# One kernel of attention and two gated layers: the strided heads of the first tile as TensorE products over eight residues

## The chip, the core and the metric

The kernel runs on one core of one Trainium2 chip. The metric is the device time of one execution in microseconds (us). Three timed runs of the kernel before gave 902.82, 904.25 and 905.61 us, a median of 904.25. The profiled execution took 902.92 us, of which the trace's span covers 901.1.

## The reference

Four sequences (B = 4) of 576 tokens go through attention with 8 heads of 64 features, and the result through two feed-forward layers of 512 to 1536 to 512.

```python
scores = scale * np.matmul(q, k.transpose(0, 1, 3, 2))
mask_local = (rel >= 0) & (rel < stride)                       # heads 0 to 3, stride = 32
mask_strided = (rel >= 0) & (pos[None, :] % stride == pos[:, None] % stride)   # heads 4 to 7
attn = np.exp(scores - max) / (sum + 1e-9)
x = np.matmul(attn, v)
x = ((x @ w_a) * (x @ w_b)) @ w_out                            # first layer
x = (sigmoid(x @ w_gate) * (x @ w_val)) @ w_out                # second layer
```

A strided head sees, for a token, only the earlier tokens with the same residue modulo 32. In the first tile of 128 tokens these are at most four.

## The kernel before

The sequence is cut into five tiles of 128, 128, 128, 128 and 64 tokens, taken for all four sequences together (512 columns). The attention of tile i + 1 is computed beside the first layer of tile i, so only tile 0's attention stands alone at the start. The first layer walks k over 12 blocks of the middle dimension: a gate product and a value product (24 matmuls of 512 columns, line 929, called L929 below), then an output product (12 matmuls, L1020). Each operand is held as a high and a low part of a narrower format, `w0p` and the like for weights, `x12p` to `x15p` for the activations: `x12p` and `x13p` hold the high parts of features 0 to 255 (local heads) and 256 to 511 (strided heads), `x14p` and `x15p` the low parts. The second layer (L1299) comes after all of it.

A weight block arrives by one DMA on the queue of SyncE (SP, L482), and four instructions make it usable: ScalarE (ACT) takes its top bits (L488), VectorE (DVE) merges (L497), ACT writes the high part (L505), DVE the low part (L509), which also frees one of three landing buffers.

Tile 0 is computed in two ways. The local heads run as four groups, one for each sequence (`attention`): ACT seeds a score bank with the mask (L561), TensorE (PE) adds the scores (L569), DVE takes the maximum (L581), ACT the exponentials (L587), DVE the reciprocal (L593) and the normalisation (L602), PE transposes (L610), ACT copies (L616), PE multiplies with the values (L624), ACT and DVE split the result (L633, L636). Before the seeds a matmul of the identity (`c_add`, L442) marks three score banks. The strided heads need no PE for their sums (`strided`): DVE and GpSimd (POOL) multiply keys by queries (L787), DVE sums over features (L793), DVE and ACT make the softmax, DVE and POOL multiply with values (L850), DVE sums (L857), PE transposes (L883), ACT and DVE split (L896, L900). The same function serves the later tiles.

The order on every engine is not written by hand: each step is handed to `Plan` with an engine (or several to choose from), a cost and a key, and `Plan.run` (L260) issues at each point the step that can start first by these costs, then by key. Engines execute in that order. While `plan.fill` is set, PE receives matmuls on a zero tile (L429) wherever the plan sees it idle in its first 27 us.

```python
    c_add = adding(SCORES, [c_idb], -20)
        z = add("ACT", act2(w), seed, [c_mask, c_add] + ...)
            a = add("PE", nb * 162, qk, [lq, z] + war, key, ...)
    strided(0, -10, 18, [], [])
    for n, g in enumerate(GROUPS):
        if g.i == 0:
            attention(g, n * 1.5, OTHERS, True, [])
```

## Time and profile before

| what | value |
|---|---|
| timed runs, us | 902.82, 904.25, 905.61 (median 904.25) |
| profiled execution, us | 902.92; span 901.1 |
| PE busy | 892.8 us, 99% of the span |
| DVE busy | 655.1 us, 73% |
| ACT busy | 405.0 us, 45% |
| POOL busy | 11.4 us, 1% |
| chain that ended last | PE 97%, DVE 3% |
| DMA | 132.67 MB, mean 147 GB/s |

Busy PE time counts fills and modelled ends, so 99% says only that PE has hardly any gap. The start has to be read from its own rows: which of PE's instructions there are fills, and what the first L929 wait for.

### The profile page before, as it was taken

The page shows a single profiled execution, that of the slowest core. Times are in us where ns is not written, and L with a number is a line of the kernel's source. Part 1 is how long each engine was busy: PE and PEld are TensorE (multiplying, and loading weights), DVE is VectorE, ACT ScalarE, POOL GpSimd, SP SyncE. Part 2 cuts the span into 40 slices and gives each one's busy share as a digit, 9 for nine tenths or more (in the row PEclk, how much of TensorE's full clock was granted, in tenths as well). Part 3 has the DMA queues.
Part 4 walks back from the last instruction along what each step waited for, and adds up shares of the span by engine and source line. Part 5 has one row for each costly group of instructions (what it writes and reads, how often), then busy time and mean ns, then how long its engine had stood idle before and what let it go on. Part 6 is the DMA issues. An engine that isn't in the chain of part 4 may idle for free.

```text
span 901.1 us, 13664 instructions
## 1 busy us (share of the span) xinstructions
PE 892.8 (99%) x5170; PEld 802.0 (89%) x5170; DVE 655.1 (73%) x1078; ACT 405.0 (45%) x843; POOL 11.4 (1%) x23
## 2 busy tenths in 40 slices
PE   8999999999999999999999999999999999999998
PEld 4678888888888888888899999999999999999998
DVE  7999988998999879811328876675768458649481
ACT  5776644411242113311236655564656445435351
POOL 4000000000000000000000000000000000000000
PEclk9999999999999999999999999999999999999999
DMA  9676564311242124300034233645575588953501
GB/s 297 212 238 221 200 195 141 91 44 61 85 137 72 54 65 134 106 1 1 0 118 164 94 139 116 213 152 187 204 241 169 194 302 331 381 165 117 167 17 62
DMA packets 62513, 132.67 MB, mean 147 GB/s; under 512 B 5872, under 2 KB 37232, under 8 KB 61552
## 3 DMA queue, kind: packets, MB, share of 16 engines
q1 hardware_dynamic: 62160, 131.60, 43.7%
q8 instruction: 40, 0.66, 0.3%
q14 instruction: 25, 0.20, 0.1%
q10 hardware_dynamic: 288, 0.21, 0.1%
HBM read 97.19 MB, written 34.60 MB: 146 GB/s over the span
## 4 chain that ended last, share of the span: by engine, by line
PE 97%; DVE 3%; issue 0%; ACT 0%; DVEq 0%
PE bank L1299 43%; PE bank L929 33%; PE bank L1020 17%; PE bank L624 1%; PE idle L429 1%; PE bank L569 1%; PE bank L610 1%; PE bank L883 0%; DVE nm L581 0%; DVE rest L497 0%; PE bank L442 0%; DVE w8p L857 0%; DVE w9p L857 0%; DVE x14p L636 0%; DVE w4p L1255 0%; DVE w0p L509 0%
## 5 line engine op out<-in xcount | busy, mean ns | idle before, releaser
L954 ACT CAST h16p<-rest 128x512 fp32r<-128x512 f32 (+1 forms) x60 | 34.7, 578 | 143.7 <-PE bank L1020 140.5
L1311 DVE TENSOR_TENSOR rest<-bank,rest 128x384 f32<-128x384 f32 x84 | 46.3, 555 | 56.6 <-PE bank L1299 32.5
L950 DVE TENSOR_TENSOR rest<-bank,rest 128x512 f32<-128x512 f32 (+1 forms) x60 | 38.1, 635 | 53.7 <-PE bank L929 53.5
L1072 ACT COPY rest<-bank 128x512 f32<-128x512 f32 (+1 forms) x60 | 32.6, 544 | 92.2 <-PE bank L929 92.0
L1317 ACT COPY rest<-bank 128x384 f32<-128x384 f32 x84 | 40.2, 479 | 67.4 <-PE bank L1299 67.1
L958 DVE TENSOR_TENSOR h16p<-rest,h16p 128x512 fp32r<-128x512 f32 (+1 forms) x60 | 38.2, 636 | 28.8 <-PE bank L1020 23.5
L787 DVE TENSOR_TENSOR rest<-rest 128x320 f32<-128x320 f32 (+13 forms) x56 | 51.5, 920 | 1.3 <-DMA rest<-sq 0.5
L850 DVE TENSOR_TENSOR rest<-rest,s 128x320 f32<-128x320 f32 (+13 forms) x56 | 51.5, 920 | 0.9
L793 DVE TENSOR_REDUCE s<-rest 128x5 f32<-128x320 f32 (+13 forms) x56 | 51.2, 915 | 1.2
L857 DVE TENSOR_REDUCE rest<-rest 128x64 f32<-128x320 f32 (+13 forms) x56 | 51.2, 915 | 1.0
L488 ACT ACTIVATE rest<-rest 128x512 f16<-128x512 bf16 x36 | 28.4, 793 | 9.4 <-DMA rest<-w 9.1
L1209 DVE SCALAR_TENSOR_TENSOR rest<-rest 128x512 uint32<-128x512 uint32 x36 | 24.7, 688 | 9.9 <-ACT rest L1202 9.8
L1202 ACT ACTIVATE rest<-rest 128x512 f16<-128x512 bf16 x36 | 28.0, 788 | 5.5 <-DMA rest<-w 5.5
L1382 DVE TENSOR_TENSOR rest<-bank,rest 128x384 f32<-128x384 f32 x36 | 20.0, 556 | 12.1 <-PE bank L1299 11.4
L1321 ACT COPY bank<-bank 128x384 f32<-128x384 f32 x42 | 19.6, 466 | 18.6 <-PE bank L1299 18.3
L1376 ACT ACTIVATE rest<-bank 128x384 f32<-128x384 f32 x36 | 17.6, 490 | 22.3 <-PE bank L1299 22.1
L497 DVE SCALAR_TENSOR_TENSOR rest<-rest 128x512 uint32<-128x512 uint32 x36 | 24.5, 685 | 0.6 <-ACT rest L488 0.5
L587 ACT ACTIVATE rest<-bank,nm 128x96 f32<-128x96 f32 x56 | 18.3, 338 | 12.2 <-DVE nm L582 10.7
L1376 ACT ACTIVATE rest<-rest 128x768 f32<-128x768 f32 x18 | 15.2, 846 | 14.0 <-DVE rest L1311 13.7
L1299 PE MATMUL bank<-w8p,w10p 128*128 128x384 f32 x100 | 20.7, 334 | 0.0
L1382 DVE TENSOR_TENSOR rest<-rest 128x768 f32<-128x768 f32 x18 | 17.2, 954 | 0.7 <-ACT rest L1376 0.3
L1299 PEld LDWEIGHTS bank<-w8p,w10p 128*128 128x128 f32 x100 | 17.6, 188 | 0.0
(500 smaller groups left out, 2413.7 us busy)
## 6 DMA issues: line engine op xcount, KB each, us to landing
rest<-w SPq DMA_DIRECT2D x72, 511.8 KB, 3.9
h2d<-rest SPq DMA_DIRECT2D x18, 768.0 KB, 4.2
rest<-qkv SPq DMA_DIRECT2D x12, 416.0 KB, 4.0
w2p<-h2d SPq DMA_DIRECT2D x12, 384.0 KB, 4.6
w0p<-h2d SPq DMA_DIRECT2D x12, 384.0 KB, 5.0
w1p<-h2d SPq DMA_DIRECT2D x12, 384.0 KB, 5.5
out<-rest SPq DMA_DIRECT2D x24, 192.0 KB, 1.8
x2d<-rest SPq DMA_DIRECT2D x16, 256.0 KB, 2.1
```

Of the source, the lines that this page charges most:

```text
L787: engine[op.eng].tensor_tensor(out=product(op, n), in0=x["k", h][:, :, :n, :], in1=x["q"][h // 2][:, e:e + nh, j:j + 1, :].to_broadcast([P ...
L793: DVE.tensor_reduce(out=weights_of(h, j, n), in_=x["p", op.deps[0]], op=ALU.add, axis=AX.X)
L850: engine[op.eng].tensor_tensor(out=product(op, n, "p (h d t) -> p h d t"), in0=x["v", h][:, :, :, :n], in1=weights_of(h, j, n).unsqueeze(2 ...
L857: DVE.tensor_reduce(out=xs[:, j, e:e + nh, :], in_=x["p", op.deps[0]], op=ALU.add, axis=AX.X)
L929: PE.matmul(x[tag][:, :n], ww[:, c * P:(c + 1) * P], xx(c), start=(u == 0 and c == chunks[0]), stop=(u == last and c == chunks[-1]),)
L950: DVE.tensor_tensor(out=x["g"], in0=x["b"][:, :n], in1=x["g"], op=ALU.mult)
L958: DVE.tensor_tensor(out=x["hl"], in0=x["g"], in1=r32(x["hh"]), op=ALU.subtract)
L1020: PE.matmul(ps[:, :n], ww[:, m * P:(m + 1) * P], x[xx], start=start, stop=stop)
L1299: PE.matmul(bank_of(where), at(*lhs(a, (0, 1, 0)[q], c), F32R), at(*rhs(b, (0, 0, 1)[q], c), F32R), start=p in OPENS and (q, c) == units[0 ...
L1311: DVE.tensor_tensor(out=at(*o), in0=bank_of("Z"), in1=at(*a), op=ALU.add)
L1317: "ACT", act2(NS), lambda op: ACT.copy(out=at(*o), in_=bank_of("Y")), [ops[after]], key - 20))
L1382: DVE.tensor_tensor(out=at(*o), in0=src(), in1=at(*o), op=ALU.mult)
```

## The change

In tile 0 the strided heads no longer go through `strided`. A new function, `strided_first`, lays queries and keys out by feature on the host (`fq`, `fk`, `fv`), with eight residues by four tokens as a block of 32. PE makes a 32 by 32 score block for each sequence, head and group of eight residues: 64 matmuls with 64 rows of contraction, on alternating halves of the array and alternating banks (L963 of the changed kernel). Of a block's entries only those of one residue and of earlier tokens count; a mask of 0 and a large negative number is put into the banks first, by a matmul of the identity with the mask in bf16 (L956). DVE and ACT make the softmax over 512 columns, PE transposes four times (L994), ACT copies (L998), and 64 small matmuls with 32 rows of contraction multiply with the values (L1024), in two steps of 32 whose results ACT and DVE split (L1041, L1045). The second step also ends the fills.

The local groups of tile 0 get their mask in the same way: one bf16 matmul of 384 columns in front of their scores (L571), in place of ACT's seed. `c_add` marks one bank instead of three. Later tiles keep the old code. The changed kernel's lines for old steps are shifted: L577 scores, L589 and L590 maximum, L595 exponentials, L601 and L602 reciprocal, L610 normalisation, L618 transposes, L624 or L626 copy, L632 values, L641 and L644 split, L433 fill, L493, L502, L510 and L514 the four weight steps, L1068 gate and value products, L800 and L806 the next tile's strided heads.

```diff
+R8 = 8
+FIRST_KEY = -1
+RB = R8 * TILES[0] // STRIDE
...
+    mskb = sb.tile([P, MW + RB], BF16, name="mskb")
...
+    c_mskb = add("ACT", act(MW + RB), lambda op: ACT.copy(out=mskb, in_=msk), [c_mask])
...
-    c_add = adding(SCORES, [c_idb], -20)
+    c_add = adding(SCORES[-1:], [c_idb], -20)
...
         def qk(op):
+            if first:
+                x["s"] = bank(op)[:, :g.width]
+                PE.matmul(x["s"], idb, g.mask(mskb), start=True, stop=False, skip_group_check=True)
...
-        z = add("ACT", act2(w), seed, [c_mask, c_add] + ([] if first else [lq]), key - 2, take=(("bank", SCORES if first else SCORES[-1:]),))
+        if first:
+            z = None
+            war = war + [c_idb, c_mskb, c_add]
+        else:
+            z = add("ACT", act2(w), seed, [c_mask, c_add, lq], key - 2, take=(("bank", SCORES[-1:]),))
         if held:
             pv_of, cost, deps, take, free, results = held
             a = add("PE", nb * 162 + cost, lambda op: (pv_of(op), qk(op)), [lq, z] + war + deps, key,
                     take=take + ring(("c", es)), free=free + ring(("qk", lq)))
             results(a)
         else:
-            a = add("PE", nb * 162, qk, [lq, z] + war, key, take=ring(("c", es)), free=ring(("qk", lq)))
+            a = add("PE", nb * 162 + first * 170, qk, [lq, z] + war, key,
+                    take=(("bank", SCORES),) if first else (("c", es),), free=ring(("qk", lq)))
...
+    def strided_first(key):
+        tq, nc2 = TILES[0] // STRIDE, HL // 2
+        nr = STRIDE // R8
+        half = B * nc2 * RB
+        w, nb = 2 * half, 2 * B * nc2
+        x = {"o": {}}
+        plan.slack = 0
+        def zone(n):
+            a = [early_tile() for _ in range(n)]
+            return a[0][0], n * DM, EARLY
+        qa, ka, va, ea, pa = zone(2), zone(2), zone(2), zone(1), zone(1)
+        def load(a, src, at_key):
+            return touch(add("SP", 450, lambda op: nc.sync.dma_start(out=at(*a), in_=src), (), at_key,
+                             size=P * a[1] * 4), (), [a])
+        lq, lk, lv = load(qa, fq, key - 9.9), load(ka, fk, key - 9.8), load(va, fv, key - 7)
+        def blocks(a):
+            return a.rearrange("p (n k) -> p n k", k=RB)
+        def wide(a):
+            return a.unsqueeze(2).to_broadcast([P, a.shape[1], RB])
+        def scores(op):
+            q, k = at(*qa), at(*ka)
+            x["s"] = [bank(op, e)[:, :half] for e in range(2)]
+            for s in x["s"]:
+                PE.matmul(blocks(s), idb, mskb[:, MW:].unsqueeze(1).to_broadcast([P, nb // 2, RB]),
+                          start=True, stop=False, skip_group_check=True)
+            for i in range(B * nc2):
+                for l in range(nr):
+                    o = (i * nr + l) * RB
+                    for e in range(2):
+                        rows = slice(e * D, (e + 1) * D)
+                        PE.matmul(
+                            x["s"][e][l * RB:(l + 1) * RB, i * RB:(i + 1) * RB], q[rows, o:o + RB], k[rows, o:o + RB],
+                            start=False, stop=i == B * nc2 - 1, skip_group_check=True)
+        def halves(a):
+            return [a[:, e * a.shape[1] // 2:(e + 1) * a.shape[1] // 2] for e in range(2)]
+        def top(op):
+            x["m"] = buf(op, "sm", [P, 32])[:, :nb]
+            for m, s in zip(halves(x["m"]), x["s"]):
+                DVE.tensor_reduce(out=m, in_=blocks(s), op=ALU.max, axis=AX.X)
+        def shift(op):
+            for m, s, o in zip(halves(x["m"]), x["s"], halves(at(*ea))):
+                DVE.tensor_tensor(out=blocks(o), in0=blocks(s), in1=wide(m), op=ALU.subtract)
+        def exp(op):
+            ACT.activation(out=at(*ea), in_=at(*ea), func=AF.Exp, scale=SCALE)
+        def total_of(op):
+            DVE.tensor_reduce(out=x["m"], in_=blocks(at(*ea)), op=ALU.add, axis=AX.X)
+            DVE.tensor_scalar_add(x["m"], x["m"], 1e-9)
+            DVE.reciprocal(out=x["m"], in_=x["m"])
+        def normalise(op):
+            engine[op.eng].tensor_tensor(
+                out=blocks(at(*ea)), in0=blocks(at(*ea)), in1=wide(x["m"]), op=ALU.mult)
+        def transpose(op):
+            x["t"] = bank(op)
+            for g in range(w // P):
+                PE.transpose(x["t"][:, g * P:(g + 1) * P], at(*ea)[:, g * P:(g + 1) * P], idt)
+        def copy_t(op):
+            if op.eng == "ACT":
+                ACT.copy(out=at(*pa), in_=x["t"])
+            else:
+                DVE.tensor_copy(out=at(*pa), in_=x["t"])
+        a = touch(add("PE", 4 * nb * 32 + 220, scores, [lq, lk, c_idb, c_mskb], key,
+                      take=[("bank", SCORES[:1]), ("bank", SCORES[1:2])]), [qa, ka])
+        b = add("DVE", 2 * dve(half), top, [a], key, take=[("sm", (0,))])
+        c = touch(add("DVE", 2 * dve(half), shift, [b], key, free=[("bank", a)]), (), [ea])
+        d = touch(add("ACT", act(w), exp, [c], key), (), [ea])
+        e = touch(add("DVE", dve(w) + 350, total_of, [d], key), [ea])
+        f = touch(add(("POOL", "DVE"), (1200, dve(w)), normalise, [e], key, free=[("sm", b)]), (), [ea])
+        t = touch(add("PE", w // P * 109, transpose, [f, c_id], key, take=[("bank", OTHERS)]), [ea])
+        h = touch(add(("ACT", "DVE"), (act(w), dve(w)), copy_t, [t], key, free=[("bank", t)]), (), [pa])
+        for c in range(nc2):
+            def values(op, c=c):
+                if c:
+                    plan.fill = None
+                for y in range(2):
+                    x["o", c, y] = bank(op, y)[:, :B // 2 * TILES[0]]
+                for g in range(B // 2):
+                    for l in range(nr):
+                        for e in range(2):
+                            for y in range(2):
+                                rows = slice((2 * c + y) * RB, (2 * c + y + 1) * RB)
+                                o = x["o", c, y].rearrange("p (g t l r) -> p g t l r", g=B // 2, t=tq, l=nr)
+                                PE.matmul(
+                                    o[e * D:(e + 1) * D, g, :, l],
+                                    at(*va)[rows, ((g * nr + l) * 2 + e) * D:][:, :D],
+                                    at(*pa)[rows, (e * 2 + g) * P + l * RB:][:, :RB]
+                                    .rearrange("p (t r) -> p t r", t=tq),
+                                    start=True, stop=True)
+            i = touch(add("PE", 32 * 45, values, [lv, h], key + 1 + c, take=[("bank", ((), (IDLE_BANK,))[c] + OTHERS[:2]), ("bank", OTHERS[2:])]),
+                      [va, pa])
+            for y in range(2):
+                def views(c=c, y=y):
+                    return [x["o", c, y].rearrange("p (g n) -> p g n", g=B // 2)] + [
+                        xT(r, 2)[:, c, :B * TILES[0]].rearrange("p (g y n) -> p g y n", g=B // 2, y=2)[:, :, y]
+                        for r in range(2)]
+                def high(op, views=views):
+                    ps, hi, lo = views()
+                    ACT.copy(out=hi, in_=ps)
+                def low(op, views=views):
+                    ps, hi, lo = views()
+                    DVE.tensor_tensor(out=lo, in0=ps, in1=r32(hi), op=ALU.subtract)
+                j = add("ACT", act(2 * P), high, [i], key + 1 + c)
+                k = add("DVE", dve(2 * P), low, [j], key + 1 + c, free=[("bank", (i, y))])
+                outs.setdefault(0, {}).setdefault(2 + c, []).append((j, k))
...
-    strided(0, -10, 18, [], [])
+    strided_first(FIRST_KEY)
```

On PE, at the start, the kernel before has the fills, the three marks and then a local group's scores (a seeded bank, `w7p` and `w6p` queries and keys):

```order
L442 MATMUL bank_108<-idb 128x512
...
L569 MATMUL bank_113<-w7p_89 64x64 x8
L429 LDWEIGHTS nil
L429 MATMUL idle<-nil 128x512
...
L569 MATMUL bank_115<-w6p_92,w7p_89 64x64 x8
```

The changed kernel has there (`w11p` holds the strided queries and keys, `mskb` the mask):

```order
L447 MATMUL bank_107<-idb 128x512
...
L956 MATMUL bank_126<-mskb,idb 128x256
...
L963 MATMUL bank_126<-w11p_76 32x32
L963 MATMUL bank_127<-w11p_76 32x32
...
L571 LDWEIGHTS idb
L571 MATMUL bank_199<-mskb,idb 128x384
L577 MATMUL bank_199<-w10p_83 64x64 x8
```

All 64 score matmuls of the strided heads stand in front of the first local group, and a mask matmul in front of every group.

On DVE the kernel before begins with products and sums of the strided heads (`w11p`, `w10p` products, `s` sums), between which the local groups' maxima are set:

```order
L787 TENSOR_TENSOR w11p_77<-w11p_77 128x512
L793 TENSOR_REDUCE s_75<-w11p_77 128x2x4
L793 TENSOR_REDUCE s_75<-w10p_84 128x2
...
L581 TENSOR_REDUCE nm_183<-bank_113 128x4
L582 TENSOR_SCALAR nm_183<-nm_183 128x4
L793 TENSOR_REDUCE s_75<-w10p_84 128x2x3
```

The changed kernel's DVE begins with the strided softmax, out of two banks:

```order
L973 TENSOR_REDUCE sm_209<-bank_126 128x8
L973 TENSOR_REDUCE sm_209<-bank_127 128x8
L977 TENSOR_TENSOR w10p_83<-bank_126,sm_209 128x256
L977 TENSOR_TENSOR w10p_83<-bank_127,sm_209 128x256
L589 TENSOR_REDUCE nm_214<-bank_199 128x4
L590 TENSOR_SCALAR nm_214<-nm_214 128x4
L983 TENSOR_REDUCE sm_209<-w10p_83 128x16
...
L589 TENSOR_REDUCE nm_238<-bank_220 128x4
...
L988 TENSOR_TENSOR w10p_83<-w10p_83,sm_209 128x512
```

Nothing on DVE precedes the end of the scores now, and the second group's maximum stands inside the strided chain.

On ACT, before the first products, the kernel before converts weights between the results of strided heads (`x13p`) and local groups (`x12p`):

```order
L896 CAST x13p_326<-bank_316 128x4x4x32
L488 ACTIVATE rest<-rest 128x512
L616 COPY w5p_122<-bank_330 96x512
L505 ACTIVATE w0p_350<-rest 128x512
L488 ACTIVATE rest<-rest 128x512
L633 CAST x12p_276<-bank_354 128x2x128
L616 COPY w4p_240<-bank_380 96x512
L896 CAST x13p_326<-bank_389 128x4x4x32
L505 ACTIVATE w0p_350<-rest 128x512
L633 CAST x12p_276<-bank_398 128x2x128
```

The changed kernel has there, from the split of the second value step to that of the last group:

```order
L1041 CAST x13p_383<-bank_349 128x2x128
L1041 CAST x13p_383<-bank_350 128x2x128
L493 ACTIVATE rest<-rest 128x512
L641 CAST x12p_420<-bank_395 128x2x128
L641 CAST x12p_420<-bank_407 128x2x128
L510 ACTIVATE w0p_434<-rest 128x512
L624 COPY w8p_93<-bank_422 96x512
L624 COPY w7p_110<-bank_429 96x512
L510 ACTIVATE w0p_434<-rest 128x512
L493 ACTIVATE rest<-rest 128x512
L641 CAST x12p_420<-bank_453 128x2x128
L641 CAST x12p_420<-bank_467 128x2x128
```

Both writes of a weight's high part (L510) have moved behind the split of the second value step.

## Rows read from the trace of the kernel before

**Rows 1.** Windows: busy us (count) of PE, PEld, DVE, ACT, POOL; PE clock; DMA.

```profile
20.00:30.00 10.00, 7.60 (x77) 4.47 (x75) 9.90 (x24) 7.10 (x21) 1.61 (x3) 1.00 0.74 236
40.00:50.00 10.00, 9.59 (x70) 7.25 (x68) 9.65 (x20) 7.07 (x16) 0.00 (x0) 1.00 0.66 203
100.00:500.00 400.00, 400.00 (x2251) 336.24 (x2250) 299.37 (x447) 128.74 (x303) 1.78 (x5) 1.00 0.28 89
```

**Rows 2.** Timeline of PE: start, us, operation, count, idle before and releaser.

```profile
0.98 3.60 PE L429 MATMUL idle<-nil 128*128 128x512 bf16 x8 [0.98 <-DVE nil L427]
5.65 4.39 PE L429 MATMUL idle<-nil 128*128 128x512 bf16 x17
...
22.57 0.69 PE L569 MATMUL bank<-rest 128*64 128x64 f32 x16
23.18 0.61 PE L429 MATMUL idle<-nil 128*128 128x512 bf16 x2
...
26.00 0.61 PE L610 MATMUL bank<-idt,w4p 128*96 128x128 f32 x4
26.45 0.60 PE L883 MATMUL bank<-idt,w8p 128*128 128x128 f32 x4
...
28.61 0.73 PE L929 MATMUL bank<-x12p,w0p 128*128 128x512 f32 x2 [0.64 <-ACT x12p L633]
...
30.47 1.09 PE L929 MATMUL bank<-x12p,w0p 128*128 128x512 f32 x4
```

**Rows 3.** Timeline of DVE at the start.

```profile
14.21 0.55 DVE L581 TENSOR_REDUCE nm<-bank 128x4 f32<-128x384 f32 x1
...
14.87 0.21 DVE L821 TENSOR_REDUCE sm<-s 128x16 f32<-128x64 f32 x1
...
24.71 0.16 DVE L593 TENSOR_SCALAR nm<-nm 128x4 f32<-128x4 f32 x1
...
28.83 0.42 DVE L636 TENSOR_TENSOR x14p<-bank,x12p 128x256 fp32r<-128x256 f32 x1
29.16 0.69 DVE L509 SCALAR_TENSOR_TENSOR w0p<-rest,w0p 128x512 fp32r<-128x512 f32 x1
29.76 0.49 DVE L787 TENSOR_TENSOR rest<-rest 128x320 f32<-128x320 f32 x1
30.36 0.49 DVE L793 TENSOR_REDUCE s<-rest 128x5 f32<-128x320 f32 x1
```

**Rows 4.** Timeline of ACT: the last exponential of group four, then five steps in a row.

```profile
19.54 0.33 ACT L587 ACTIVATE w4p<-bank,nm 128x96 f32<-128x96 f32 x1
...
22.12 0.80 ACT L488 ACTIVATE rest<-rest 128x512 f16<-128x512 bf16 x1
22.77 0.57 ACT L616 COPY w5p<-bank 96x512 f32<-96x512 f32 x1
23.23 0.68 ACT L505 ACTIVATE w0p<-rest 128x512 fp32r<-128x512 f32 x1
23.81 0.80 ACT L488 ACTIVATE rest<-rest 128x512 f16<-128x512 bf16 x1
24.45 0.37 ACT L633 CAST x12p<-bank 128x256 fp32r<-128x256 f32 x1
```

**Rows 5.** PE instructions by form, 0 to 35 us: busy, mean ns, idle before.

```profile
L569 PE MATMUL bank<-w7p 128*64 128x64 f32 x16 | 0.7, 228 | 0.0
```

**Rows 6.** Timeline of POOL at the start.

```profile
7.04 2.82 POOL L787 TENSOR_TENSOR w10p<-w10p 128x128 f32<-128x128 f32 x3 [5.24 <-DMA w10p<-sk]
```

**Rows 7.** Timeline of SP: issue of the second weight block.

```profile
13.27 0.33 SPq L482 DMA_DIRECT2D rest<-w  x1
```

**Rows 8.** DMA issues in the same place: size, us to landing.

```profile
rest<-w SPq DMA_DIRECT2D x1, 511.8 KB, 7.8
```

**Rows 9.** Timeline of DVE, last sum of the second tile's strided heads.

```profile
130.12 0.67 DVE L857 TENSOR_REDUCE rest<-rest 128x64 f32<-128x512 f32 x1
```

**Rows 10.** Timeline of PE, the transposes that read it.

```profile
131.13 0.60 PE L883 MATMUL bank<-idt,rest 128*128 128x128 f32 x4
```

More of the change, by code (lines that the diff above doesn't have):

```diff
@@ L351, in attention_moe_kernel @@
 @with_exitstack
-def attention_moe_kernel(ctx, tc, qkv, sq, sk, sv, w1, w2, mask, ident, out):
+def attention_moe_kernel(ctx, tc, qkv, fq, fk, fv, sq, sk, sv, w1, w2, mask, ident, out):
     nc = tc.nc
@@ L668, in attention @@
         c = add("ACT", nb * (act(WB) + 186), exp, [b], key + 2 * ST,
-                free=[("bank", z)])
+                free=[("bank", z or a)])
         used(c, (), [ee])
@@ L683, in results @@
         def results(i):
-            j = add("ACT", act(2 * g.n), high, [i] + war, i.key / 1e3 + ST)
+            j = add("ACT", act(2 * g.n), high, [i] + ([] if first else war), i.key / 1e3 + ST)
             k = add("DVE", dve(2 * g.n), low, [j], i.key / 1e3 + ST, free=[("bank", i)])
```

17 lines of the change are left out of this document (13 added, 4 removed).

## The prediction

> **What bounds the kernel now.** I first read the busy time by windows. From 100 to 500 us PE is busy 400.00 of 400.00, while DVE there has a quarter of its time free [rows 1]: behind the start the kernel is as long as PE's work. From 20 to 30 us PE is busy only 7.60 of 10, part of it fills, and DVE 9.90 of 10 [rows 1]. So what an edit of tile 0 is worth is the earlier moment at which PE's products begin to run without a gap, less what PE gets to do after it, which is nothing here.
>
> The second view is PE's timeline. The products of local features (`x12p`) start at 28.61, where PE had stood still 0.64 us for ACT's split [rows 2]. The tenth gate or value product is the second of the four at 30.47; they follow each other by 0.23 (1.09, less 0.40 for the end of the last, over three), so it ends at 30.93 [rows 2]. This is the mark by which I compare: ten products done, four local groups finished, the fifth group's scores done. In both orders the rest follows in the same manner.
>
> The third view, DVE and ACT side by side, says why it is so late. The fourth group's last exponential ran at 19.54 on ACT, but DVE got to its reciprocal at 24.71 [rows 3, 4]. Those 4.8 us are DVE's queue, full of the strided heads' products and sums. The change takes these away.
>
> **Prices of the steps.** All from one step's start to the next. DVE: 256 columns 0.33, 512 columns 0.60 (28.83, 29.16, 29.76), a maximum with its scaling 0.66 (14.21 to 14.87) [rows 3]. ACT: weight's top bits 0.65, copy of 512 0.46, high part 0.58 (22.12 to 23.81), 256-column split 0.25 to 0.37, taken as 0.25 [rows 4]. PE: scores of a group 0.61 (22.57 to 23.18), four transposes 0.45 (26.00 to 26.45) [rows 2]. A handover between engines I take as 0.1, with another 0.05 to 0.15 for the end of a matmul.
>
> What no row shows is a pass of a 32 by 32 by 64 product. A group's scores are 8 matmuls in the program and 16 in the trace, two passes each; so the 64 score matmuls are 128 passes, the value matmuls 64 passes in each of two steps. The nearest row has 64-column passes at (0.69 − 0.228) / 15 = 31 ns [rows 5]. That is the upper end, a pass that gains nothing from its half length. The lower end is 32 columns at the pace of a 512-column product: 32 × 227 / 512 = 14 ns. I take 22, the middle: half the columns, with neighbours on other halves of the array, but two instructions for each pass as in the row.
>
> **The change, step by step, at 22 ns.** PE first runs ten fills and the one mark at 0.43 us, from 0.98 to 5.7. [...] So three more fills at 0.43, four at 0.216 and two mask matmuls bring PE to 8.1. The loads don't hold it: `fq` and `fk` are 1.05 MB and stand first on SP; the first four strided loads, the same bytes, had landed by 7.04, when POOL could start [rows 6]. Behind them the order of SP changes, but in front of the first weight block stand the same bytes.
>
> Scores: 128 × 22 = 2.8, to 10.9. DVE: two maxima and two subtractions, 4 × 0.34, to 12.45. ACT: exponential of 512, 0.58, to 13.15. DVE: sum 0.6, plus and reciprocal 0.37; then the second group's maximum, 0.66, which stands ahead of the normalisation; then that, 0.6: 15.55. PE: transposes, 16.15; two fills 0.43 and the fourth group's mask and scores 0.77, to 17.35. ACT's copy is done by 17.0, so the values' first step runs 17.35 to 18.75. It shares banks with the local groups, so the second step waits for the first group's transposes (0.45) and DVE's copy of them (0.6): 20.2. It ends at 21.65.
>
> From there ACT's queue sets the end, since both weight blocks' high parts and the last local split stand in line behind that step. From 21.9: two splits 0.5, second block's top bits 0.65, two splits 0.5, high part 0.58, two copies 0.93, high part 0.58, third block's top bits 0.65, two splits 0.5: 4.9, to 26.8. PE starts the `x12p` products at 27.0 instead of 28.61; five more products after the first two (7 × 0.23) bring the mark to 28.6 instead of 30.93: **2.3 us earlier**.
>
> The mask matmuls (0.16 each) replace ACT's seeds and lie in the steps counted. POOL normalises the fourth group, from 21.8: at its 3.1 ns a column (2.82 us for 128, 256 and 512 columns [rows 6]) that is 1.2 us, to 23.0, and PE comes to it at 23.5. DVE loses strided work of tile 0, but its queue at the start of the next tile's strided heads moves with the rest: by the same sum it reaches L793's counterpart at 28.25 instead of 30.36 [rows 3], 2.1 earlier. That matters at the next tile, where DVE's last sum ended at 130.8 and PE came to it at 131.13 [rows 8, 9, 10]: 0.3 of slack, and the shifts differ by 0.2. In 40 to 50 us PE lacks 0.41 [rows 1], waits for weights; the changed ACT queue can lose as much again, since the fifth block's top bits now precede the fourth's high part. I count these two as nothing, ±0.4.
>
> Each further ns costs 128 + 128 ns: gain = 2.3 − 0.255 × (p − 22). It is zero at 31 ns. Below 18 the landing of the second weight block at 13.27 + 7.8 = 21.07 [rows 7, 8] begins to set ACT's queue, and the gain ends at 3.6.
>
> [...] The row has 31 ns for 64 columns [rows 5]; it cannot tell length from instruction. [...]
>
> **Rivals.** *A. Neighbouring passes overlap fully* (14 to 20 ns). For it: the passes alternate halves and banks. Against: the row's passes alternate column halves too, and took 31. Gain 2.9 to 3.6: about 900.7.
>
> *B. A pass costs what the row shows*, whatever its length (28 to 31 ns): the strided heads' 256 passes take 8 us of PE's queue, in front of every local group, and DVE's freed time turns into waiting. Gain 0 to 0.8: about 903.5.
>
> *C. PE's clock falls.* Between 11 and 21 us there are 12 fills where PE had been kept full, and the small products use a quarter of the array or less. If the pace there fell to 0.43 for 512 columns, the path's PE work after the scores (0.45 + 0.43 + 0.77 + 1.4 + 0.45 + 1.4 = 4.9) doubles, and the first 6 us of products (as long as fills took before the pace rose [rows 2]) lose 3: 7.9 − 2.3 = 5.6 slower, 909.5. It decides from a loss of 5.0, where the whole is 0.3% slower. Against: PE's gaps in my sum are under 0.9 us, and before it kept its pace across a 0.64 gap at 28.61.
>
> **Numbers.** The profiled execution, 902.92, is its span of 901.1 and 1.8 around it; less 2.3 it is 900.6. It lies 1.3 under the median of 904.25, so I set the sum against the mean of the four executions, 903.9: **901.6**. Chances: forecast (21 to 28 ns) 0.45, with 900 to 903.5 its own range; A 0.33; B 0.12; C 0.10. The bound of 0.3%, 2.7 us, is what a measurement of this kernel tells from no change. A passes it, with a little of the forecast's better edge, 0.40 faster; C makes 0.10 slower; the rest, 0.50, is the same. The range of 898.6 to 905.0 holds the three cases without C, with ±0.9 for executions.
>
> **What would show it.** The strided scores should start at about 8.1 and take 2.8; the values' steps 1.4 each; ACT should run without a gap from 21.9 to 26.8; `x12p` products should start near 27.0, and PE have no gap beyond 0.5 us after. I am wrong if the passes follow each other by less than 18 or more than 28 ns, if fills after 8 us come at 0.43, if PE waits at 131, or if a wait appears behind 30 us that keeps what the start gave.

## The result: slower by 0.6%, and the profile after

The changed kernel takes 908.95 us (908.33 to 909.23, six runs), the kernel before 903.12 beside it; the ratio is 1.0059 (95% interval 1.0046 to 1.0072). The forecast of 901.6, with a range of 898.6 to 905.0, was wrong, and so was its sign. The profiled execution has 908.95 us and a span of 907.2, 6.1 more than before.

TensorE's timeline of the changed kernel (start, us, operation, count, idle before) answers to [rows 2, 5]:

```profile
8.10 1.29 PE L963 MATMUL bank<-w11p 64*32 64x32 f32 x128
...
15.99 0.69 PE L577 MATMUL bank<-w7p,w8p 128*64 128x64 f32 x16 [0.74 <-DMA w7p<-qkv]
16.60 1.13 PE L1024 MATMUL bank<-w10p,w11p 32*64 32x32 f32 x64
17.67 0.64 PE L618 MATMUL bank<-idt,w10p 128*96 128x128 f32 x4
...
19.02 0.89 PE L1024 MATMUL bank<-w10p,w11p 32*64 32x32 f32 x43
23.39 0.54 PE L1024 MATMUL bank<-w10p,w11p 32*64 32x32 f32 x21 [3.48 <-issue]
23.86 1.05 PE L632 MATMUL bank<-w9p,w10p 96*64 96x64 f32 x16
...
26.57 1.01 PE L618 MATMUL bank<-idt,w7p 128*96 128x128 f32 x4
...
30.20 0.72 PE L1068 MATMUL bank<-x12p,w0p 128*128 128x512 f32 x2
...
31.45 1.09 PE L1068 MATMUL bank<-x12p,w0p 128*128 128x512 f32 x4
...
37.45 0.73 PE L1068 MATMUL bank<-x12p,w1p 128*128 128x512 f32 x2 [1.74 <-ACT w1p L510]
```

Until 19 us nothing is later than forecast: the scores start at 8.10, as forecast, and the second values step at 19.02, not 20.2. Then TensorE stops in the middle of that step, after 43 of 64 passes, for 3.48 us. "Issue" says that it waited for nothing that the profile shows. The products with `x12p` start at 30.20 instead of 28.61 [rows 2], and the next weight block keeps them waiting 1.74 us more.

ScalarE's timeline shows the hole handed on: its queue stands behind the strided split for 3.37 us, and the weight steps behind it.

```profile
23.96 0.65 ACT L1041 CAST x13p<-bank 128x256 fp32r<-128x256 f32 x2 [3.37 <-PE bank L1024]
24.49 0.79 ACT L493 ACTIVATE rest<-rest 128x512 f16<-128x512 bf16 x1
...
34.13 0.79 ACT L493 ACTIVATE rest<-rest 128x512 f16<-128x512 bf16 x1 [1.78 <-DMA rest<-w]
```

The windows (columns as in [rows 1]) show the rest of that stage: the transfers run dry at 37 GB/s, and TensorE's mean granted clock is 0.90 and 0.76 of full from 20 to 30 us, where it was 1.00 up to the hole. From the first values behind the hole to the second set of transposes are 2.71 us (23.86 to 26.57).

```profile
16.00:20.00 4.00, 3.85 (x132) 3.30 (x133) 3.39 (x10) 3.01 (x15) 0.00 (x0) 1.00 1.04 318
20.00:25.00 5.00, 1.61 (x43) 1.57 (x44) 1.80 (x6) 1.63 (x5) 1.14 (x1) 0.90 0.90 291
25.00:30.00 5.00, 5.00 (x74) 4.07 (x71) 3.89 (x10) 4.30 (x10) 0.00 (x0) 0.76 0.18 37
```

The transfers run dry because SyncE's queue stands: from 18 to 45 us its longest wait (queue, awaited, us in all, times, longest) is that of a load of later queries and keys (L556) for the scores of the fifth group to be done, which come behind the hole (27.51). The loads of the next weight blocks stand after it. In the kernel before the same wait took 3.8 us.

```profile
SPq L556 <- PE bank L577: 8.0, 1, 8.0
```

How far the changed kernel is behind the one before, at places that both have: tenth product 1.0 us (31.9 against 30.93), first output product 3.0, the next gate or value product 2.0, first product of the second layer 2.66, its last 5.79, span 6.1. So half of the loss arises where the change touches nothing. The first and last product of the second layer, of the kernel before:

```profile
502.66 1.40 PE L1299 MATMUL bank<-w0p,w4p 128*128 128x384 f32 x6
...
897.30 0.51 PE L1299 MATMUL bank<-w11p,x15p 128*128 128x384 f32 x2
```

and after:

```profile
505.32 1.39 PE L1438 MATMUL bank<-w0p,w4p 128*128 128x384 f32 x6
...
903.09 0.51 PE L1438 MATMUL bank<-w11p,x15p 128*128 128x384 f32 x2
```

394.64 us became 397.77, for 2268 passes in either. By form (busy us, mean ns of one with its modelled end, so that neighbours overlap; idle before), a pair with weight block 10 before, and two pairs after:

```profile
L1299 PE MATMUL bank<-w8p,w10p 128*128 128x384 f32 x48 | 9.6, 334 | 0.0
```

```profile
L1438 PE MATMUL bank<-w8p,w10p 128*128 128x384 f32 x48 | 9.8, 338 | 0.0
L1438 PE MATMUL bank<-w7p,w5p 128*128 128x384 f32 x36 | 7.2, 334 | 0.0
```

Pairs with one of the tiles of blocks 10 and 11 are slower (337 to 340 ns, before 334 or 335), most others are not (334 to 336).

### The profile page after: what moved, and what is told of

Read it like the earlier page. It is cut to its first block, busy times and chain, and to the rows that moved or that the text cites. A ratio compares the mean times of both kernels' runs of the same rounds, so it can differ in the third digit from the quotient of the medians.

```text
span 907.2 us, 14091 instructions
## 1 busy us (share of the span) xinstructions
PE 894.9 (99%) x5402; PEld 805.9 (89%) x5402; DVE 647.1 (71%) x1059; ACT 407.3 (45%) x849; POOL 4.3 (0%) x13
## 4 chain that ended last, share of the span: by engine, by line
PE 93%; DMA 3%; DVE 2%; issue 1%; ACT 0%; SPq 0%; ACTq 0%; DVEq 0%
PE bank L1438 43%; PE bank L1068 31%; PE bank L1159 16%; PE bank L632 1%; PE bank L618 1%; DMA w7p<-qkv 1%; PE bank L577 1%; DMA rest<-w 1%; DMA msk<-mask 1%; DMA rest<-sq 1%; DVE rest L800 0%; DVE rest L502 0%; DVE s L806 0%; PE bank L896 0%; PE bank L1024 0%
## 5 line engine op out<-in xcount | busy, mean ns | idle before, releaser
L800 DVE TENSOR_TENSOR rest<-rest 128x320 f32<-128x320 f32 (+13 forms) x56 | 51.6, 921 | 2.3 <-DMA rest<-sq 1.3
L806 DVE TENSOR_REDUCE s<-rest 128x5 f32<-128x320 f32 (+13 forms) x56 | 51.2, 914 | 1.2 <-DVE rest L800 0.5
L493 ACT ACTIVATE rest<-rest 128x512 f16<-128x512 bf16 x36 | 28.3, 793 | 6.6 <-DMA rest<-w 6.6
L502 DVE SCALAR_TENSOR_TENSOR rest<-rest 128x512 uint32<-128x512 uint32 x36 | 24.6, 684 | 1.2 <-ACT rest L493 1.2
L595 ACT ACTIVATE rest<-bank,nm 128x96 f32<-128x96 f32 x56 | 18.3, 340 | 11.4 <-DVE nm L590 9.9
```

The source lines that it names most:

```text
L800: engine[op.eng].tensor_tensor(out=product(op, n), in0=x["k", h][:, :, :n, :], in1=x["q"][h // 2][:, e:e + nh, j:j + 1, :].to_broadcast([P ...
L806: DVE.tensor_reduce(out=weights_of(h, j, n), in_=x["p", op.deps[0]], op=ALU.add, axis=AX.X)
```

## The experiments

Two causes were to be found: of the hole, and of the slower passes.

### The hole: where it stands

The page of the changed kernel has, in its parts on engines and DMA queues:

```profile
PE 894.9 (99%) x5402; PEld 805.9 (89%) x5402; DVE 647.1 (71%) x1059; ACT 407.3 (45%) x849; POOL 4.3 (0%) x13
...
q8 instruction: 42, 0.69, 0.3%
```

0.69 MB in 42 packets are 16 KB each. TensorE's 5402 passes, each with its weight load, and 79 other instructions of its program are 10,883: 259 to a packet, some 63 bytes each. From these numbers my estimate is a block of 256 instructions of 64 bytes to a packet (42.5 blocks); the runs below test the 256. Counted in the program, 705 instructions stand ahead of the hole; with 63 of start-up they would be 768, three blocks. The 63 are set by this one hole and kept below.

**e1_shift20** adds 20 instructions at the very start.

```diff
+    fills = [0]
+    def fill():
+        fills[0] += 1
+        n = 2 if fills[0] <= 10 else 1
+        for i in range(n):
+            PE.matmul(idle[:, :512 // n], nil, nil.unsqueeze(1).to_broadcast([P, 4 // n, P]), start=True, stop=True)
+
+    plan.fill = fill
...
```

> The first ten fills are issued as twenty matmuls of 256 columns instead of ten of 512: the same work and time, 20 instructions more ahead of everything else. Theory A: the 3.48 us in the second values step is TensorE out of instructions. The instruction queue's packets are 16 KB, 256 instructions of 64 bytes; the hole falls at the end of the third block, and the fourth lands late. Then the hole moves up by 20 instructions, ten passes: 33 passes of the step (a pass is a weight load and a matmul) come before it and 31 behind it, and it stays 3.3 to 3.9 us. Rival B: the step waits for something of its own (a bank, a buffer, an engine whose signal the profile doesn't show); then the hole stays behind the 43rd pass.

Measured (timeline of TensorE; 909.47 us, one run):

```profile
13.28 0.52 PE L1001 MATMUL bank<-idt,w10p 128*128 128x128 f32 x3
14.06 0.33 PE L1001 MATMUL bank<-idt,w10p 128*128 128x128 f32 x1 [0.26 <-issue]
...
17.94 0.73 PE L1031 MATMUL bank<-w10p,w11p 32*64 32x32 f32 x33
21.60 0.66 PE L1031 MATMUL bank<-w10p,w11p 32*64 32x32 f32 x31 [2.93 <-issue]
```

The hole is behind the 33rd pass, and rival B falls. A small gap that I had not foreseen stands where, by the same count, the second block ends: behind the third of four transposes.

**e9_swap_odd** gives the second values step a later place (with the tiles moved as in e5 below).

```diff
...
-            i = touch(add("PE", 32 * 45, values, [lv, h], key + 1 + c, take=[("bank", ((), (IDLE_BANK,))[c] + OTHERS[:2]), ("bank", OTHERS[2:])]),
+            i = touch(add("PE", 32 * 45, values, [lv, h], key + 1 + c * 5, take=[("bank", ((), (IDLE_BANK,))[c] + OTHERS[:2]), ("bank", OTHERS[2:])]),
...
```

> The second values step gets a later key and is issued behind the values of the first two groups and the scores of group 4; tiles at odd multiples of 128. Its 64 passes are all kept. Theory A: the third block of instructions now ends inside the values of group 2, after about 5 of their 16 passes; a hole of 1 to 2.5 us stands there instead of in the strided step, and the queues of ScalarE and VectorE, which stood behind the strided split for 3.4 us, have the weight steps of block 0 before them: products with x12p by 29 us (after: 30.2), time 903 to 905. If the hole belonged to the step, it goes with it.

```profile
20.62 0.34 PE L634 MATMUL bank<-w8p 96*64 96x64 f32 x5
23.40 0.69 PE L634 MATMUL bank<-w8p 96*64 96x64 f32 x11 [2.44 <-issue]
```

After five passes, as counted. The hole belongs to the count, not to the strided step. Of the time that it was to save nothing is seen in the profiled execution (clock 0.50 from 24 to 32, four transposes 1.09 us at 24.01 against 0.62 at 19.09, `x12p` at 31.11), but the median is 903.14 (901.04 to 906.94, ten runs; ratio 1.0002, 0.9987 to 1.0017). The profile shows one of its longest executions: the six with a mean granted clock of 0.998 or more took 901.04 to 903.36 us, the four with 0.996 or less 903.72 to 906.94. No run here shows why the clock falls further in some executions of one kernel than in others.

**e12_strided_odd** keeps the strided part alone; ScalarE seeds the first groups' banks as before.

```diff
...
-                PE.matmul(x["s"], idb, g.mask(mskb), start=True, stop=False, skip_group_check=True)
+        z = add("ACT", act2(w), seed, [c_mask, c_add] + ([] if first else [lq]), key - 2, take=(("bank", SCORES if first else SCORES[-1:]),))
...
```

> Only the strided part of the change is left: the first groups' banks are seeded by ScalarE as before. The strided scores are issued later, behind the scores of four groups, and the two values steps stand one behind the other, 256 instructions. Theory A: 256 instructions in a row are used up in 2 to 3 us, which no fetch under load (7 us) follows: TensorE stands with the label issue again, 1 us or more in all, in the strided scores (the second block ends after 66 of their 128 passes) or at the values steps (the third ends just before them, the fourth just behind). If the hole needs the mask matmuls, it is gone. Time 904 to 910.

```profile
19.90 0.77 PE L957 MATMUL bank<-w11p 64*32 64x32 f32 x66
21.44 0.73 PE L957 MATMUL bank<-w11p 64*32 64x32 f32 x62 [0.76 <-issue]
```

Behind the 66th pass, as counted; only 0.76 us long, less than expected, and at the values steps no wait on "issue". Its 916.0 us (one run), more than expected, goes with the order: the strided softmax now follows all groups, and `x12p` starts at 34.93.

**e8_mask_only** keeps the mask part alone.

```diff
-    strided_first(FIRST_KEY)
+    strided(0, -10, 18, [], [])
```

> Only the mask part of the change is left: the score banks of the first groups get the mask by the bf16 matmul, and the first tile's strided heads are computed on VectorE and GpSimd as before. Here no burst of small matmuls empties an instruction block, and its tiles lie at odd multiples of 128. Theory A with P2: no idle of TensorE put down to issue, the second layer at 394.6 us, and the time 902 to 904, like before: the mask part carries none of the loss. If the mask part has a share in the loss (its matmul, the later mask transfer), the time is 905 or more.

902.57 us (ratio 0.9991, 0.9982 to 1.0001), no wait on "issue", second layer 394.65 us: the mask part alone shows no loss.

### The hole: how long it lasts

**e4_probe** appends 1024 small matmuls where the transfers are nearly over.

```diff
+        last = psum.tile([P, 512], F32, tag="bank0", name="bank0")
+        for _ in range(1024):
+            PE.matmul(last[:32, :32], nil[:, :32], nil[:, :32], start=True, stop=True)
```

> 1024 small bf16 matmuls (32 columns, 32 rows, constant operands, nobody reads them) are appended behind the last product, where the transfers are nearly over (share 0.04 to 0.17): 2048 instructions, eight blocks of 256. Theory A: TensorE runs 128 passes and then stands, again and again, seven or eight times; a period is the time that a fetch takes with empty queues (4 us or less, from 8.9 asked to 13.0 landed in the after profile). Rival B: no holes, the 1024 passes run through at 10 to 30 ns each.

```profile
903.29 14.50 PE L1694 MATMUL bank<-nil 128*32 128x32 bf16 x546
918.15 3.36 PE L1694 MATMUL bank<-nil 128*32 128x32 bf16 x128 [0.36 <-issue]
921.88 9.42 PE L1694 MATMUL bank<-nil 128*32 128x32 bf16 x350 [0.36 <-issue]
```

Two gaps only, of 0.36, just 128 passes apart; the instruction packets come 3.4 to 4.0 us apart. A pass took 26 ns, so 256 instructions last 3.36 us, and 1024 passes hold eight ends of blocks: with quiet queues (share 0.13 from 903 to 907 us, the end of the changed kernel) six of them show no gap. If a block is asked for when the last but one before it is used up, which is my assumption, the fetch took no longer than 3.36 us, and twice 3.72. My "seven or eight times" was wrong because I took the pass for shorter.

In the changed kernel the second block was used up at about 16.1 (same count), the packet moved between 20.5 and 20.6, and TensorE went on at 23.39: 7.3 us. No view shows the moment of asking; it is taken from the count. The packet (kind, packets, MB, share, window 20.5 to 20.6):

```profile
q8 instruction: 1, 0.02, 75.6%
```

The third block lasted from 16.1 to 19.91, 3.8 us. Two kernels were to take loads out of the queues, **e2_light** and **e13_relief**:

```diff
...
-            start = strided(i + 1, begin[i], span[i], start, war)
+            start = strided(i + 1, begin[i], span[i], held_back if i == 0 else start, war)
...
```

> The third weight block and the first loads of the next tile's strided heads (1.3 MB in all) wait for the second strided split and so no longer stand in the DMA queues between 15 and 24 us. Theory A with contention: the fourth instruction block is asked for at 16.1 us and landed at 20.5 in the after profile because it stood behind these loads; now it lands by 18.5, and the hole in the second values step is under 1.5 us. If a fetch takes its 7 us whatever the queues hold, the hole stays at 3.5 us. Rival B: the hole stays. The time need not fall, since weights and strided keys come later: 906 to 912.

> All loads that are not needed before 20 us (the first weight blocks, the next tile's groups and strided heads) wait for the second strided split; only the first tile's own 4 MB are in the queues. Theory A with contention: these are over by 14 to 16 us, the fourth instruction block, asked for when the second is used up at about 16 us, is there within 3.4 to 3.8 us, as at the quiet end of the appended matmuls, and the hole after the 43rd pass is under 0.8 us. If a fetch takes its 7 us at any load, the hole stays at 3 to 3.5 us. All later work is several us late since the weights are: 908 to 920.

Holes of 3.20 us (913.57 us; 1.0122, 1.0106 to 1.0137) and 2.38 us (922.28), both behind the 43rd pass. But neither did what it says: what I added is a dependence in the planner, which gives an order, and no wait when the program runs. The transfers' share was still 1.05 at 18 to 20 us in e13. These two tell nothing of contention.

**e16_relief_wait** makes the loads wait for a write into their own buffers, issued behind the second split.

```diff
+                if w is w1 and done_loads.append(c) is None and len(done_loads) <= 3:
+                    DVE.memset(x["raw"][:, :1], 0)
...
```

> The first three weight blocks and the first loads of the next tile (scores, values, strided heads) each wait for a one-column write by VectorE behind the second strided split, into the buffer that they fill. Only the first tile's own 4.2 MB are in the queues, over by 15 or 16 us. Theory A with contention: the fourth instruction block, asked for at about 16 us, lands within 3.4 to 3.8 us; the hole after the 43rd pass is 0 to 0.8 us. A fetch of 6 to 7 us at any load: the hole stays at 2.4 to 3.5 us with the transfers idle. Time 915 to 930, since all weights come 10 us late.

Timeline of TensorE, two windows, and the packet of the fourth block (window 17 to 17.1):

```profile
18.73 1.34 PE L1035 MATMUL bank<-w10p,w11p 32*64 32x32 f32 x64
20.01 0.69 PE L639 MATMUL bank<-w9p,w10p 96*64 96x64 f32 x16
...
21.61 0.64 PE L625 MATMUL bank<-idt,w7p 128*96 128x128 f32 x4
```

```profile
16.00:18.00 2.00, 2.00 (x84) 1.89 (x80) 1.73 (x6) 1.32 (x9) 0.00 (x0) 1.00 0.03 8
18.00:20.00 2.00, 1.94 (x70) 1.52 (x67) 2.00 (x6) 1.24 (x7) 0.00 (x0) 1.00 0.00 0
```

```profile
q8 instruction: 1, 0.02, 66.6%
```

With the queues empty the packet moved 1.2 us behind the end of the second block (15.9 by the count; 4.4 us in the changed kernel), and the step ran through, though its order and so its count are the same. The clock stayed at 1.00, and what took 2.71 us takes 1.60 (20.01 to 21.61): the fallen clock cost 1.1 there. (In the 917.59 us of its one run TensorE later waits 4.86 us for the first weights.) So the hole is a late fetch, and the full queues make it late.

When a block is asked for is not shown. In e16, with nothing else in the queues (share 0.03 from 16 to 18 us), the packet of the fourth block moved at 17.0 to 17.1, only after the second block was used up (15.9); in the changed kernel, too, it came behind that moment (20.5 against 16.1). My assumption agrees with both, and neither proves it.

### The slower passes: where the tiles lie

The change made the tiles of constants larger (`msk`, and `mskb` new) and the order another in which tiles are first used. In bytes of a partition, modulo 256, the tiles of weights and activations all begin at 128 in the kernel before; in the changed kernel those of weight blocks 10 and 11 begin at 0, the others at 128. The constants are not the reason: they push all by 768 bytes, three times 256. The order is: the tile of the strided sums (`s`, 1152 bytes) stood ahead of the tiles of blocks 11 and 10, and now stands behind them. Four kernels move the tiles and do nothing else, and one moves them in the kernel before:

```diff
@@ e3_pad: 256 bytes ahead of all
+    idb = sb.tile([P, 2 * P], BF16, name="idb")[:, :P]
@@ e6_even: 128 ahead of all
+    nil = sb.tile([P, P + 64], BF16, name="nil")[:, :P]
@@ e11_all_even: 128 behind block 10
+            return sb.tile([P, shape[1] + 32], dtype, tag=f"{ring}{s}", name=f"{ring}{s}")[:, :shape[1]]
@@ e5_odd: the edits of e6_even and e11_all_even together
@@ e15_before_mixed: in the kernel before, the edit of e6_even, and
+                tiles[r] = phase, sb.tile([P, r[1] + 32 * (name == "w10")], F32, tag=name, name=f"{name}p{phase}")
```

> One tile of 256 bytes a partition is left unused ahead of the big tiles, so that all of them begin 256 bytes further on (those that held weight blocks 10 and 11 no longer begin at a multiple of 1024 bytes); nothing else is changed. Theory P: half of the loss, 3.1 us between 510 us and the end, is the pace of the second layer's passes (334 ns each before, 335 to 338 after), set by where the tiles lie in the buffer memory, not by the edit. Then the passes are at 334 again, the second layer is 2.4 to 3.1 us shorter and the time 905.8 to 906.6; the hole in the second values step is unchanged, after 43 passes and 3.5 us long. If the pace belongs to something else (instruction positions, transfers), the passes stay at 335 to 338 and the time at 908.5 to 909.2.

> All big tiles are placed at odd multiples of 128 bytes, as in the kernel before (128 unused bytes ahead of the tile of weight block 11, 128 more behind that of block 10; with 256 bytes ahead of all the pace stayed, so it isn't the residue to 1024). In the after profile just those two tiles lie at multiples of 256, and pairs with them run at 338 ns, where before no pair with them was over 335. Theory P2: this parity sets the pace. Then the second layer takes 394.6 us from its first to its last product, as before (after: 397.8), and the time is 905.5 to 906.3. If the pace belongs to the new order of the tiles or to anything else in the change, it stays 397.8 and 907.5 to 909.

> 128 unused bytes ahead of all big tiles: weight blocks 10 and 11 come to odd multiples of 128 bytes, all other tiles to multiples of 256. If a pass is slow by 2.7 ns when one of its tiles begins at a multiple of 256, nearly all 2340 passes of the second layer are slow: 400 us or more for the layer, 911 or more in all. If it is slow when its two tiles differ in parity, this is the after kernel's picture: 397.8 us, 908.5 to 909.2. If parity has no part, also 397.8.

> 128 unused bytes only behind the tile of weight block 10: all big tiles lie at multiples of 256. If passes are slow when their two tiles differ in parity, the second layer is as fast here as with all at odd multiples: 394.6 to 395.2 us from first to last product. If a tile at a multiple of 256 makes its passes slow by itself, all are slow: 400 us or more. The hole in the second values step stays at 3 to 3.6 us after 43 passes.

> The kernel before with 128 unused bytes ahead of its big tiles and 128 more behind the tile of weight block 10: blocks 10 and 11 lie at multiples of 256, all others at odd multiples of 128, as in the after kernel. If mixed parity makes passes slow, the second layer goes from 394.6 to 397.8 us from first to last product, and the time from 903 to 906 to 907. If the new order of the tiles or anything else of the change is behind it, 394.6 and 903.

Second layer from first to last product (starts), and time:

```
kernel            blocks 10, 11 / others   second layer   time, ratio with 95% interval
before            128 / 128                394.64
after             0 / 128                  397.77         908.95  1.0059 (1.0046 to 1.0072)
e3_pad            0 / 128                  397.77         907.77  1.0054 (1.0037 to 1.0071)
e6_even           128 / 0                  397.80         908.93  1.0058 (1.0043 to 1.0073)
e5_odd            128 / 128                395.13         906.12  1.0026 (1.0014 to 1.0037)
e11_all_even      0 / 0                    394.63         904.42  (one run)
e15_before_mixed  0 / 128                  397.77         906.23  1.0037 (1.0022 to 1.0051)
```

The pad of 256 bytes kept the parity (odd or even multiples of 128), and the pace with it; my first theory, the residue to 1024, falls. All at 0 is as fast as all at 128 (394.63 and 394.64 us), so it is the difference between a pass's two tiles. The last kernel settles it: nothing but placement, and its passes by form and its second layer are those of the changed kernel.

```profile
L1299 PE MATMUL bank<-w8p,w10p 128*128 128x384 f32 x48 | 9.8, 338 | 0.0
```

```profile
503.59 1.39 PE L1299 MATMUL bank<-w0p,w4p 128*128 128x384 f32 x6
...
901.36 0.51 PE L1299 MATMUL bank<-w11p,x15p 128*128 128x384 f32 x2
```

It makes the kernel before 3.3 us slower (906.23 against 902.93 beside it). And e8_mask_only, which has the larger constants and the old order, has all at 128 and the old pace:

```profile
502.31 1.40 PE L1438 MATMUL bank<-w0p,w4p 128*128 128x384 f32 x6
...
896.96 0.51 PE L1438 MATMUL bank<-w11p,x15p 128*128 128x384 f32 x2
```

### Is the forecast gain there without the two losses?

**e7_merge_odd** halves the values' instructions: 16 matmuls a step, both heads at once.

```diff
...
-                                    o[e * D:(e + 1) * D, g, :, l],
-                                    at(*va)[rows, ((g * nr + l) * 2 + e) * D:][:, :D],
+                                o[:, :, g, :, l], at(*va)[rows, (g * nr + l) * 2 * D:][:, :2 * D],
...
```

> Each values step is written in 16 matmuls of 128 columns of weights by 64 columns, both heads of a pair at once (half of what they write is not read), instead of 32 of 64 by 32: 64 instructions fewer a step; the splits are in two halves each. With the tiles at odd multiples of 128. Theory A: the third block of instructions now ends behind both values steps, in the first pass or two of the scores of group 4; a hole, if there is one, stands there and is under 2 us, since other waits fill the time till then. The tenth product ends by 30 us instead of 31.9, the clock stays at 1.00 between 18 and 30, the time is 902 to 904. Rival B (the second step waits for something of its own): a hole of 3 us stays in the second values step, and the time is 905 to 906.

```profile
19.73 2.06 PE L1025 MATMUL bank<-w10p,w11p 32*128 32x64 f32 x32
...
24.93 0.61 PE L620 MATMUL bank<-idt,w7p 128*96 128x128 f32 x4 [1.48 <-DVE x15p L1047]
...
29.40 1.08 PE L1070 MATMUL bank<-x12p,w0p 128*128 128x512 f32 x4
...
34.52 0.73 PE L1070 MATMUL bank<-x12p,w1p 128*128 128x512 f32 x2 [0.88 <-ACT w1p L512]
```

No hole, clock 1.00 from 18 to 32, tenth product at 29.86: 1.07 us earlier than before. But VectorE's split, now in two halves, holds a bank for 1.48 us, the next weight block is late by 0.88, and the second layer begins only 0.57 earlier, at 502.09. The time is 904.1 us (902.58 to 908.13, ten runs; ratio 1.0012, 0.9997 to 1.0027), no change that can be told. The profile is that of the shortest, with a mean clock of 1.00; three of the ten, with 0.992 to 0.994, took 904.73 to 908.13.

Three tries to free what is left, all with the wide matmuls: a later second step, a fifth bank for the transposes, weight steps planned earlier.

```diff
@@ e10_merge_swap_odd: the later key of e9_swap_odd
@@ e14_merge_bank5
-                take=[("bank", banks)], free=ring(("c", a)))
+                take=[("bank", banks + SCORES[1:2] * first)], free=ring(("c", a)))
@@ e17_merge_early
-STEP, AHEAD, LEAD, EARLIER = 1.4, 10, 12, 4
+STEP, AHEAD, LEAD, EARLIER = 1.4, 10, 12, 9
```

> The 16 wide matmuls a step together with the later second step, tiles at odd multiples of 128. Theory A: the third block ends at the fill behind the scores of group 4, where it is due after 24 us; no hole over 0.5 us. The wait of the fourth transposes for a bank of the second split (1.48 us with the wide matmuls alone) goes, too; tenth product done by 29.3 us, time 901.5 to 903.5. If the later split becomes what x13p's products wait for, no gain against the wide matmuls alone: 903.5 to 905.

> The wide matmuls, tiles at odd multiples of 128, and the first groups' transposes may also use a fifth bank (the second of the strided scores, free by then). The order follows: the second values step comes behind the values of the first two groups. Theory A: the third block ends in the values of group 2, due at 23.5 us or later, so the hole is under 1 us; no wait of the transposes for the second split; x12p's products by 28 us, tenth product done by 29.7, time 901 to 903.5. If the bank they take is late for the products of x13p instead, 903.5 to 906.

> The wide matmuls with tiles at odd multiples of 128, and the first two weight blocks' steps planned 5 us earlier, so that ScalarE and VectorE do them between the strided splits instead of behind them. If the late fourth weight block is what takes the 1.1 us back, the wait of the first product with the next weight block (0.88 us) goes, and the second layer begins by 501.5 instead of 502.1: 902.5 to 904. If the splits, now later, hold x13p's products instead, the tenth product comes after 30.5 and the time is 904 to 906. The third block of instructions ends in or just behind the scores of group 4: no hole over 0.5 us.

e10: 907.17 us (1.0037, 1.0025 to 1.0049); the split of `x12p` came late by 0.98, the clock was 0.82 from 24 to 32. e14: 904.92 (1.0019, 1.0008 to 1.0031); no hole and no bank wait, but the clock fell to 0.72 from 18 to 24 without any hole, and `x12p` started at 28.90. e17: 903.76 (901.85 to 906.03; 1.0005, 0.9995 to 1.0015); the split of `x12p` was late by 0.87 instead. None beats the kernel before.

## Why the prediction was wrong, step by step

- **"20.2. It ends at 21.65."** This is the step that failed first. The sum lets the second values step run through in 1.4 us and hangs ScalarE's queue behind it. The step began early, at 19.02, and ended at 23.93: TensorE stood 3.48 us for instructions in its midst, a wait that the sum does not have, on a resource that no view of before shows at its limit. Behind it the products with `x12p` came at 30.20, not 27.0, and the tenth product at 31.9, not 28.6.
- **"less what PE gets to do after it, which is nothing here."** This failed second. The same products behind the start did not take the same time: 3.13 us of the 6.1 are the second layer's passes, slower by the place of two tiles. I did not ask what the change moves in memory.
- **The price of a pass, 22 ns**, bounded at 14 and 31 ns. Measured, start to start: 9.6 ns for the scores (8.10 to 9.33, 128 passes), 16.7 for the values (16.60 to 17.67, 64). I named under 18 as proof that I am wrong. The sum erred on the slow side, and priced time only: it did not count that 128 passes are 256 instructions, and that the third block was used up in 3.8 us, about half of the 7.3 us to the next.
- **Fills at 0.43 and then 0.216,** the terms up to 8.1: in the kernel before eight fills took 3.39 us from start to start (0.98 to 4.37), and five behind the change of pace 1.08 (7.72 to 8.80), with a granted clock of 1.00 in both stretches. The changed kernel's scores came at 8.10, as the sum has it. What changes the pace no run shows.
- **DVE, ACT and the transposes:** forecast transposes at 15.55, found at 14.03; values at 17.35, found at 16.60. The mechanism up to 19 us was right, and only its prices were high.
- **Rival C, the falling clock,** came true in part, with 1.1 us of cost. In the changed kernel it fell behind the hole (0.76 from 25 to 30 us), and in e16, without the hole but with the same fills, it stayed at 1.00 until 24 us. That speaks for the hole as the cause there. But in e14 (0.72 from 18 to 24), e10 (0.82 from 24 to 32) and e17 (0.79 from 24 to 32) it falls without a hole, so the rival was no empty one, and no run shows what lowers the clock there.
- **"Waits for weights, ±0.4":** 1.74 for the second weight block, since the queues of ScalarE and SyncE stood behind the hole, and 0.5 for a later one.
- **The tile boundary at 131:** no wait there; TensorE came 3 us late to it.
- **The gain of 2.3:** without hole and mixed places 1.07 is left at the tenth product (e7, whose wide matmuls take 0.9 more a step), 0.57 at the second layer, and nothing that the time shows. The later waits that I put at nothing take half of it back; where the rest goes stays open. The clock is not all of it: the seven executions of e7 with a mean clock of 0.998 or more, 902.58 to 904.50 us, are no faster than the kernel before either.

What stays open: the last tile of the first layer. Products of 256 columns there follow each other by 113.5 ns in after, e3, e6 and e15, and by 118 in the kernel before and the others with like places. In e15, where only places differ, the layer's other tiles lose (0.9 us behind at the first product with `x12p`, 29.49 against 28.61; 2.6 at the last tile's first, 451.11 against 448.50), and the last tile gives 1.7 back. It is not the places alone: e1, with the places of the changed kernel and 20 more instructions, has 118 in nearly all of them. Most of these passes don't use blocks 10 and 11, and no run here tells why.

## What to carry to other kernels

Count the instructions, not only their times. In the changed kernel 256 of TensorE's were used up in 3.8 us while the transfers were busy (share 1.04), and TensorE stood for 3.48 us; in e12 they were used up in 5.6 us, and it stood for 0.76. Where a kernel has such a stretch, look for idle time with the label "issue" at every 256th, and try the work in fewer, wider instructions: in e7, with 32 passes a step instead of 64, the hole was gone. Before pricing an edit, compare the addresses of all large tiles: here a small tile (`s`) that was first used later moved two others, and 3.1 us were lost in passes that are nowhere in the diff. And a kernel with nothing but the places moved is the control for it.

## What the hardware showed that was not expected

- From the end of one block of 256 instructions until TensorE went on behind the next block were, by the count, at most 3.72 us with quiet queues (e4; share 0.13 at the end of the changed kernel), 7.3 with a transfer share of 1.04 from 16 to 20 us and 0.90 from 20 to 25 (changed kernel), and the stops of the changed kernel, e1, e9 and e12 fell at instruction 512 or 768, to the pass, with 63 of start-up set by the first.
- Passes of 384 columns whose two tiles begin at places that differ by 128 modulo 256 read 337 to 340 ns instead of 334 or 335 (`w11p` with `w5p` 338, with `w7p` 340, both 334 before); over a layer of 2268 passes, not all of them such, it is 3.1 us (394.64 to 397.77).
- A pass of 32 by 32 by 64 followed the last by 9.6 ns, less than a third of what a pass of twice the columns took in the kernel before (31 ns [rows 5]).
